# Both groups of heads in one pass of the packing stage, with the first batch ahead of everything else

## The chip, the cores and the metric

The kernel runs on one core of a Trainium2 chip. The metric is the device time of one execution in microseconds (us); lower is better. The engines are named as in the profile: PE is TensorE, which multiplies, PEld its weight loads, DVE is VectorE, ACT is ScalarE, POOL is GpSimd, and SP is the queue that issues nearly all DMAs.

## The reference

Three layers follow each other on 8 batches of 576 tokens with 512 features (8 heads of 64).

```python
# 1. packed attention, per batch and head: p has 32 rows of 64
p_packed = softmax(p @ k.T / 8) @ v
out = softmax(q @ p_packed.T / 8) @ p_packed
# 2. four causal attention experts with 64 features, the two best per token by x @ w_gate
x = concat of the heads
y_e = softmax(causal(x @ wq[e] @ (x @ wk[e]).T / 8)) @ (x @ wv[e]) @ wo[e]
out = sum over the two chosen experts of gate weight * y_e
# 3. token-shift feed-forward
xk = mu_k * x + (1 - mu_k) * x_prev;  xr = mu_r * x + (1 - mu_r) * x_prev
return sigmoid(xr @ w_r) * ((maximum(xk @ w_k, 0) ** 2) @ w_v)
```

## The kernel before, in words

Each batch has two groups of four heads (`NG = 2`). The generator `front(b, g)` takes one group through the packed attention, in nine pieces that end with `yield`: load p, k, v, q (L220 to L229); scores p by k (`heads`, L231), their maximum and exponential (L233 to L238); transposes of the exponentials (L245) and their copy `aT`; the product with v (L254) and its scaling `pp` (L262); the transpose of `pp` and its copy `ppT`; scores q by packed p, transposed on DVE into `st` (L275), maximum `m` (L278), subtraction on POOL (L279), exponential (L280); the product of `ppT` with the weights `wa` of the next layer, kept as a high part `PWh` (L283) and a low part `PWl` (L284); the sums (L287), reciprocal and scaling of `st`; the transpose `a` (L294), kept as `A2h` (ACT) and `A2l` (POOL).

`project` (L374) multiplies `A2h`, `A2l` by `PWh`, `PWl` of both groups into queries and keys, `values` (L319) into values and gate scores. For each expert `soft` makes the causal scores (PE L437), masks and reduces them on DVE (L449) and takes the exponential on ACT (L453); `turn` transposes them (L469, L476), `pair_out` multiplies by the values (L514). Beside this run `fold`, which multiplies `wo` into `w_k` and `w_r` (PE L638), and `vweights`. Both read weights through `decode`: five DVE instructions for each 128 x 256 piece (L568 to L582; the DMA target is `raw`), one on ACT, one on POOL. After the eight batches come `rstage`, `kstage` and `vstage` (L761, L783, L816) over six blocks of columns.

What stands where on an engine is set in two steps. `steps` holds pairs of a time and a generator, and the sorted list calls `next` on them; the times of `front` are `FRONT_T`, shifted by `G1_T` for the second group. The framework then lists the instructions of each engine by its own estimate of when they are ready, and by a priority (`PR` by kind). At run time each engine works through its list in order: an instruction that waits holds all behind it. The DMA queue SP too is such a list.

`pT`, `kT` and the PSUM tiles `big` have two buffers each, the PSUM tiles `one` four. `vn` is two fixed tiles.

Of the kernel before, what the change touches and what calls it, by code (L numbers as in the profile page):

```python
# [23 lines left out]
FRONT_T = [-29.42, -25.75, -23.2, -18.64, -17.38, -14.9, -12.54, -11.97, -8.22]  # L24
G1_T = [1.16, 2.9, 3.77, 1.72, 1.63, 2.21, 3.77, 1.1, 3.2]
VAL_T = [-1.16, -1.09, -0.83, 0.03, 0.74]
PROJ_T = [-1.82, -1.2, 2.22, 2.78]
GROUPS = ((0, 3), (1, 2), (4,))
SOFT_T = [1.34, 2.42, 3.15]
TURN_LAG = [4.17, 4.87, 5.4]  # L30
OUT_LAG = [3.85, 4.62, 7.81]
FOLD_T = [-27.87, 10.28, 107.76]
FOLD_N = 13
V_END = -11.02
WA_AT = -24.33
WR_AT = 8.0
R_LOAD, R_RUN = [14.0, 15.0], [22.0, 28.0]
E_R = "PV"
W_AT = [2.2, 4.2, 5.2]
# [8 lines left out]
PR = {"front": 0, "values": -100, "project": 0, "soft": 0, "turn": 0, "out": 100, "fold": 0, "v": -70, "k": 0, "gates": 0}  # L48
# [7 lines left out]
def kernel(  # L56
# [81 lines left out]
    if True:  # L138
# [17 lines left out]
        vns = [ld.tile([P, NT, 4 * D], F32, name=f"vn{x}", bufs=1) for x in range(2)]  # L156

# [36 lines left out]
        def heads(lhs, rhs, n):  # L194

            ps = big()
            for h in range(4):
                for x in range(2):  # L200
                    nc.tensor.matmul(
                        ps[32 * h : 32 * h + 32, 512 * x : 512 * x + n],
                        lhs[64 * x : 64 * x + 64, 32 * h : 32 * h + 32],
                        rhs[64 * x : 64 * x + 64, h, :],
                        start=True, stop=True,
                    )
            return halves(ps)[:, :, :n]

        def front(b, g):


            if g == 0:
                bats[b] = {
                    n_: bt.tile([P, NG, w], F32R, tag=n_, name=nm(n_))
                    for n_, w in (("A2h", S), ("A2l", S), ("PWh", NQK), ("PWl", NQK))
                }
            bat = bats[b]
            pT = fr.tile([P, P], F32, tag="pT", name=nm("pT"))
            for x in range(2):
                nc.sync.dma_start(pT[64 * x : 64 * x + 64], p[b, g])  # L220
            kT = ld.tile([P, 4, SH], F32, tag="kT", name=nm("kT"))
            nc.sync.dma_start(kT, k[b, g])
            vn = vns[(b * NG + g) % 2]
            nc.sync.dma_start(
                vn[:, : NT - 1, :], v[b, g, : (NT - 1) * P].rearrange("(c p) x -> p c x", p=P)
            )
            nc.sync.dma_start(vn[TAIL:, NT - 1, :], v[b, g, (NT - 1) * P :])
            qT = ld.tile([P, 4, SH], F32, tag="qT", name=nm("qT"))
            nc.sync.dma_start(qT, q[b, g])  # L229
            yield  # L230
            s1 = heads(pT, kT, SH)  # L231
            mx = sm.tile([P, 1], F32, tag="mx1", name=nm("mx1"))
            nc.vector.tensor_reduce(mx, s1, op=ALU.max, axis=AX.XY)  # L233
            nb = sm.tile([P, 1], F32, tag="nb1", name=nm("nb1"))
            nc.vector.tensor_scalar(nb, mx, -SC, None, op0=ALU.mult)
            a1 = fr.tile([P, S], F32, tag="sa", name=nm("a1"), bufs=4)
            su = sm.tile([P, 1], F32, tag="su1", name=nm("su1"))
            nc.scalar.activation(halves(a1), s1, AF.Exp, bias=nb, scale=SC, accum_out=su)  # L238
            nc.vector.tensor_scalar(su, su, EPS, None, op0=ALU.add)
            ri = sm.tile([P, 1], F32, tag="ri1", name=nm("ri1"))  # L240
            nc.vector.reciprocal(ri, su)
            yield
            ps = big()
            for c in range(NT):
                nc.tensor.transpose(  # L245
                    ps[:, c * P : (c + 1) * P], a1[:, start(c) : start(c) + P], ident
                )
            aT = fr.tile([P, NT, P], F32, tag="aT1", name=nm("aT1"), bufs=1)
            evac(E_AT, aT.rearrange("p c q -> p (c q)"), ps[:, : NT * P])
            yield  # L250
            ps = one()
            for c in range(NT):
                for h in range(4):
                    nc.tensor.matmul(  # L254
                        ps[32 * h : 32 * h + 32, :D],
                        aT[:, c, 32 * h : 32 * h + 32],
                        vn[:, c, D * h : D * h + D],
                        start=c == 0, stop=c == NT - 1,
                    )

            pp = fr.tile([P, P], F32, tag="pp", name=nm("pp"))
            nc.vector.tensor_scalar(  # L262
                pp.rearrange("p (x d) -> p x d", x=2),
                ps[:, :D].unsqueeze(1).to_broadcast([P, 2, D]), ri, None, op0=ALU.mult,
            )
            yield
            ps = one()
            nc.tensor.transpose(ps[:, :P], pp, ident)
            ppT = fr.tile([P, P], F32, tag="ppT", name=nm("ppT"))
            evac(E_PPT, ppT, ps[:, :P])  # L270
            yield
            s2 = heads(ppT, qT, SH)
            st = fr.tile([P, S], F32, tag="sa", name=nm("st"), bufs=4)
# [664 lines left out]
```

## Time and profile before

| | |
|---|---|
| median of 3 runs | 873.24 us (871.94 to 873.52) |
| the profiled execution | 872.8 us, its span 871.0 us |
| PE busy | 801.6 us (92% of the span) |
| DVE busy | 548.2 us (63%) |
| POOL, ACT busy | 381.5 us (44%), 377.0 us (43%) |
| DMA | 115.37 MB, mean 132 GB/s; 305 GB/s in the first fortieth of the span |

The span is the time from the first instruction to the last; the run's own time has 1.8 us around it. Busy shares are averages over stages that differ: PE is busy for all of the last 320 us but for about half of the first 44. The clock column (PEclk) gives the share of full speed that was granted; TensorE has two levels, 1.2 and 2.4 GHz. "Idle before" in brackets is the time an engine stood still before an instruction, and what released it.

### The profile page before, as it was taken

The page shows a single profiled execution, that of the slowest core. Times are in us where ns is not written, and L with a number is a line of the kernel's source. Part 1 is how long each engine was busy: PE and PEld are TensorE (multiplying, and loading weights), DVE is VectorE, ACT ScalarE, POOL GpSimd, SP SyncE. Part 2 cuts the span into 40 slices and gives each one's busy share as a digit, 9 for nine tenths or more (in the row PEclk, how much of TensorE's full clock was granted, in tenths as well). Part 3 has the DMA queues.
Part 4 walks back from the last instruction along what each step waited for, and adds up shares of the span by engine and source line. Part 5 has one row for each costly group of instructions (what it writes and reads, how often), then busy time and mean ns, then how long its engine had stood idle before and what let it go on. Part 6 is the DMA issues. An engine that isn't in the chain of part 4 may idle for free. (4 is left out here: it accounts for less than half of the span.)

```text
span 871.0 us, 16389 instructions
## 1 busy us (share of the span) xinstructions
PE 801.6 (92%) x6112; PEld 658.2 (76%) x6112; DVE 548.2 (63%) x1246; ACT 377.0 (43%) x936; POOL 381.5 (44%) x517
## 2 busy tenths in 40 slices
PE   4588999989999889899898978999999999999998
PEld 2285866859678586667777867998889888898896
DVE  2779578694895888986674775554454644554342
ACT  2337657676675856868556453211212112021120
POOL 5773566455763845545443252332423223232230
PEclk9999998999999999999999999999999999999999
DMA  8745461654635467340545875023121131120401
GB/s 305 257 138 167 142 198 63 182 147 128 216 115 161 144 193 212 97 117 24 155 147 186 293 298 209 4 86 108 49 85 62 62 132 49 73 73 1 145 1 72
DMA packets 65903, 115.37 MB, mean 132 GB/s; under 512 B 6048, under 2 KB 45472, under 8 KB 65696
## 3 DMA queue, kind: packets, MB, share of 16 engines
q1 hardware_dynamic: 65824, 114.33, 40.3%
q8 instruction: 48, 0.79, 0.4%
q14 instruction: 31, 0.25, 0.1%
HBM read 71.32 MB, written 33.55 MB: 120 GB/s over the span
## 5 line engine op out<-in xcount | busy, mean ns | idle before, releaser
L816 PE MATMUL one<-wvh,kk 128*128 128x512 f32 x576 | 187.6, 393 | 0.1
L192 POOL TENSOR_TENSOR kk<-y,kk 128x768 fp32r<-128x768 f32 x48 | 89.9, 1873 | 213.7 <-ACT kk L796 213.7
L816 PEld LDWEIGHTS one<-wvh,kk 128*128 128x128 f32 x576 | 107.5, 188 | 22.6 <-DVE rr L821 0.5
L816 PE MATMUL one<-wvl,kk 128*128 128x512 f32 x288 | 113.2, 394 | 0.0
L453 ACT ACTIVATE ms<-ms,nb 64x64 f32<-64x64 f32 (+4 forms) x160 | 89.4, 560 | 32.2 <-DVE nb L449 29.7
L796 ACT CAST kk<-y 128x768 fp32r<-128x768 f32 x48 | 40.1, 836 | 133.0 <-DVE y L794 96.6
L744 DVE TENSOR_TENSOR y<-big,p 128x256 f32<-128x256 f32 x48 | 20.3, 423 | 116.1 <-POOL kk L192 100.3
L185 ACT COPY tb<-one 64x128 f32<-64x128 f32 (+5 forms) x208 | 65.9, 356 | 22.1 <-PE one L469 19.5
L791 ACT COPY p<-big 128x256 f32<-128x256 f32 x48 | 17.9, 373 | 125.0 <-PE big L783 106.2
L514 PE MATMUL one<-tb,vg 128*64 128x320 f32 (+4 forms) x448 | 62.1, 379 | 3.2 <-ACT p L767 2.3
L816 PEld LDWEIGHTS one<-wvl,kk 128*128 128x128 f32 x288 | 54.1, 188 | 10.4
L449 DVE CUSTOM_DVE_ANT_0 ms<-one,mstrip 64x64 f32<-64x64 f32 (+3 forms) x128 | 51.3, 420 | 13.1 <-PE one L437 10.9
L469 PE MATMUL one<-ident,ms 128*128 128x128 f32 x320 | 55.6, 286 | 3.7 <-ACT ms L453 2.4
L514 PEld LDWEIGHTS one<-tb,vg 128*64 128x64 f32 x448 | 37.2, 142 | 26.0 <-issue 3.6
L469 PEld LDWEIGHTS one<-ident,ms 128*128 128x128 f32 x320 | 37.3, 143 | 23.1 <-issue 10.7
L821 DVE TENSOR_TENSOR rr<-one,rr 128x512 f32<-128x512 f32 x36 | 23.1, 683 | 41.2 <-PE one L816 41.1
L794 DVE SCALAR_TENSOR_TENSOR y<-y 128x768 f32<-128x768 f32 x48 | 48.0, 999 | 1.6
L181 POOL TENSOR_SCALAR dh<-dl 128x2048 fp32r<-128x2048 f32 x10 | 19.2, 1923 | 65.2 <-DMA dl<-dscr 65.2
L437 PE MATMUL one<-ks,qs 128*128 128x64 f32 (+3 forms) x128 | 41.0, 345 | 5.6 <-DVE tb L187 2.6
L578 POOL TENSOR_TENSOR dcx<-dcx,dce 128x256 f32<-128x256 f32 x40 | 29.3, 733 | 38.2 <-DVE dce L575 32.7
L476 PE MATMUL one<-ident,ms 128*128 128x128 f32 x160 | 35.6, 287 | 9.9 <-DVE nb L449 6.0
L739 DVE TENSOR_TENSOR dl<-dl,dh 128x2048 fp32r<-128x2048 f32 x10 | 29.7, 2971 | 18.2 <-POOL dh L181 18.2
(172 smaller groups left out, 2086.2 us busy)
## 6 DMA issues: line engine op xcount, KB each, us to landing
dl<-dscr SPq DMA_DIRECT2D x10, 1024.0 KB, 6.1
kT<-in_k_dram SPq DMA_DIRECT2D x16, 576.0 KB, 4.6
qT<-in_q_dram SPq DMA_DIRECT2D x16, 576.0 KB, 5.4
rscr<-rr SPq DMA_DIRECT2D x12, 768.0 KB, 4.1
rr<-rscr SPq DMA_DIRECT2D x12, 768.0 KB, 4.3
out_dram<-rr SPq DMA_DIRECT2D x11, 768.0 KB, 3.3
vn<-in_v_dram SPq DMA_DIRECT2D x16, 512.0 KB, 5.0
dscr<-dt SPq DMA_DIRECT2D x16, 384.0 KB, 4.6
```

Of the source, the lines that this page charges most:

```text
L185: nc.scalar.copy(o, x)
L192: nc.gpsimd.tensor_tensor(o, x, y, op=op)
L437: nc.tensor.matmul(ps[:, po : po + kn], qs[:, i * P : i * P + P], keys[:, ko : ko + kn], start=x == 0, stop=x == 1,)
L449: nc.vector.tensor_tensor_reduce(halves(mv) if last else mv, sv, halves(mk) if last else mk, op0=ALU.add, op1=ALU.min, scale=-SC, scalar=3 ...
L453: nc.scalar.activation(mv, mv, AF.Exp, bias=nb[p0:], scale=-1.0, accum_out=bat["sums"][p0:, i, e : e + 1],)
L469: nc.tensor.transpose(ps[:, at + j * P : at + (j + 1) * P], ms[:, j * P : (j + 1) * P], ident)
L476: nc.tensor.transpose(pd[:, at + P * x : at + P * x + P], ms[:, start(i) : start(i) + P], ident)
L514: nc.tensor.matmul(av[64 * ee : 64 * ee + 64, qo - lo : hi - lo], vg[:, j, HD * (2 * ep + ee) : HD * (2 * ep + ee + 1)], tslice(tabs[ee], ...
L739: nc.vector.tensor_sub(dl, f32(dl), f32(dh))
L794: nc.vector.scalar_tensor_tensor(y, y, 0.0, y, op0=ALU.max, op1=ALU.mult)
L796: nc.scalar.copy(kk[:, 0], y)
L816: nc.tensor.matmul(ps, kk[:, a, x, t0 : t0 + P], wres["v"][b][:, f, :], start=n == 0, stop=n == 3 * NFT - 1,)
```

## The change

`front(b)` now takes both groups through each piece together: every tile is a list of two, and each step is written for group 0 and then for group 1. `st`, `a1`, `aT` and `a2` share four buffers of one tag. `tc.issue_after` asks that PE work of a piece stand behind that of the piece before. For the first batch three things differ: its priority is 1000 in place of 0 (`PR0`); the four small loads of p are issued by ACT and not by SP; and the subtraction, the scaling and the `A2l` subtraction go to DVE and not to POOL (`light`), which moves six instructions. At the start DVE clears a one-column tile `warm`, ACT takes its exponential, and PE multiplies 16 times a 128 x 128 piece of zeros of `mstrip` (`WARM`), all at the highest priority. In `pair_out` the two experts of a pair change places. The times of many steps are other numbers.

```diff
-FRONT_T = [-29.42, -25.75, -23.2, -18.64, -17.38, -14.9, -12.54, -11.97, -8.22]
-G1_T = [1.16, 2.9, 3.77, 1.72, 1.63, 2.21, 3.77, 1.1, 3.2]
+FRONT_T = [-25.49, -24.5, -21.5, -17.8, -16.5, -14.0, -11.0, -10.5, -7.0]
...
+PR0, WARM = 1000, 16
...
+        with tc.high_priority(offset=10000):
+
+            warm = const.tile([P, 1], F32, name="warm")
+            nc.vector.memset(warm, 0.0)
+            nc.scalar.activation(warm, warm, AF.Exp)
+            wps = one()
+            for _ in range(WARM):
+                nc.tensor.matmul(wps[:, :P], mstrip[:, :P], mstrip[:, P : 2 * P], start=True, stop=True)
...
+            gs = range(NG)
+            light = nc.gpsimd if b else nc.vector
+
+            def wide():
+                return [fr.tile([P, NT * P], F32, tag="sa", name=nm("sa"), bufs=4) for _ in gs]
...
+                for x in range(2):
+                    (nc.sync if b else nc.scalar).dma_start(pT[g][64 * x : 64 * x + 64], p[b, g])
+                kT.append(ld.tile([P, 4, SH], F32, tag="kT", name=nm("kT")))
+                nc.sync.dma_start(kT[g], k[b, g])
...
+            s1 = [heads(pT[g], kT[g], SH)[0] for g in gs]
+            a1, mx, nb, su, ri = wide(), small("mx1"), small("nb1"), small("su1"), small("ri1")
+            for g in gs:
+                nc.vector.tensor_reduce(mx[g], s1[g], op=ALU.max, axis=AX.XY)
+                nc.vector.tensor_scalar(nb[g], mx[g], -SC, None, op0=ALU.mult)
+                nc.scalar.activation(
+                    halves(a1[g][:, :S]), s1[g], AF.Exp, bias=nb[g], scale=SC, accum_out=su[g]
+                )
+            yield
+            for g in gs:
+                nc.vector.tensor_scalar(su[g], su[g], EPS, None, op0=ALU.add)
+                nc.vector.reciprocal(ri[g], su[g])
...
+            for g in gs:
+                for hf in range(2):
+                    nc.vector.transpose(st[g][:, SH * hf : SH * hf + SH], s2[g][:, hf, :])
+                nc.vector.tensor_reduce(m2[g], st3[g], op=ALU.max, axis=AX.X)
+                light.tensor_tensor(
+                    st3[g], st3[g], m2[g].unsqueeze(2).to_broadcast([P, NCB, NPK]), op=ALU.subtract
+                )
+                nc.scalar.activation(st[g][:, :S], st[g][:, :S], AF.Exp, scale=SC)
...
+                light.tensor_tensor(
+                    st3[g], st3[g], r_[g].unsqueeze(2).to_broadcast([P, NCB, NPK]), op=ALU.mult
+                )
+            yield
+            a2 = wide()
+            for g in gs:
+                nc.vector.transpose(a2[g][:, :S], st[g][:, :S])
+                evac(E_AH, bat["A2h"][:, g, :], a2[g][:, :S])
+                light.tensor_tensor(
+                    bat["A2l"][:, g, :], a2[g][:, :S], f32(bat["A2h"][:, g, :]), op=ALU.subtract
+                )
...
-                    for ee in range(2):
+                    for ee in (1, 0):
...
-            for g in range(NG):
-                add("front", front(b, g), [t0 + t + g * G1_T[i] for i, t in enumerate(FRONT_T)])
+            add("front", front(b), [t0 + t for t in FRONT_T], None if b else PR0)
```

Three places in the engines' lists show what this moves. Line numbers of the changed kernel are its own; `sa` there is what was `a`, `aT` or `st`.

First, the head of SP's list before, up to the first weight piece `raw`:

```order
L220 DMA pT_130<-in_p_dram 64x128 x2
L222 DMA kT_133<-in_k_dram 128x1152
L224 DMA vn_122<-in_v_dram 128x4x256
L227 DMA vn_122<-in_v_dram 64x256
L229 DMA qT_137<-in_q_dram 128x1152
L220 DMA pT_139<-in_p_dram 64x128 x2
```

and of the change:

```order
L240 DMA kT_170<-in_k_dram 128x1152
L240 DMA kT_175<-in_k_dram 128x1152
L243 DMA vn_122<-in_v_dram 128x4x256
L247 DMA vn_122<-in_v_dram 64x256
L249 DMA qT_179<-in_q_dram 128x1152
L243 DMA vn_123<-in_v_dram 128x4x256
```

The loads of p have left the list, and both loads of k stand first; behind these rows the same loads follow in the same order as before, up to `wa` and `raw`.

Second, DVE in the first batch from the first piece of `raw` on, before:

```order
L568 TENSOR_SCALAR dce_233<-raw_230 128x256
L571 SCALAR_TENSOR_TENSOR dcx_232<-raw_230,dce_233 128x256
L574 TENSOR_SCALAR dce_233<-dcx_232 128x256
L275 STREAM_TRANSPOSE st_342<-big_333 128x288 x2
L575 SCALAR_TENSOR_TENSOR dce_233<-raw_230,dce_233 128x256
L278 TENSOR_REDUCE m_57_345<-st_342 128x18
L582 SCALAR_TENSOR_TENSOR sq_229<-sq_229,dcx_232 128x256
```

and of the change, where `sa_370` and `sa_371` are `st` of the two groups and `big_352`, `big_361` their scores:

```order
L305 STREAM_TRANSPOSE sa_370<-big_352 128x288 x2
L306 TENSOR_REDUCE m_59_372<-sa_370 128x18
L305 STREAM_TRANSPOSE sa_371<-big_361 128x288 x2
L606 TENSOR_SCALAR dce_241<-raw_238 128x256
L307 TENSOR_TENSOR sa_370<-sa_370,m_59_372 128x576
L306 TENSOR_REDUCE m_60_373<-sa_371 128x18
L609 SCALAR_TENSOR_TENSOR dcx_240<-raw_238,dce_241 128x256
L317 TENSOR_TENSOR PWl_166<-big_398,PWh_165 128x772
```

The transposes and the first maximum have gone ahead of the first decode instruction, all later work of the batch still stands behind it, and the subtractions are new in DVE's list. From `dce_241<-raw_238` to the second `A2l` the changed list has 30 instructions.

Third, DVE in the fifth batch, where the next scores of `soft` (ISA `ms`) meet the maxima of the two groups, before:

```order
L233 TENSOR_REDUCE mx_558_2708<-big_2699 128x1
L575 SCALAR_TENSOR_TENSOR dce_3408<-raw_3405,dce_3408 128x256
L235 TENSOR_SCALAR nb_559_2710<-mx_558_2708 128x1
L294 STREAM_TRANSPOSE a_566_2733<-st_2477 128x576
L239 TENSOR_SCALAR su_561_2713<-su_561_2713 128x1
L241 RECIPROCAL ri_562_2716<-su_561_2713 128x1
L568 TENSOR_SCALAR dce_3501<-raw_3498 128x256
L531 TENSOR_TENSOR cb_2724<-one_2668,cb_2724 128x320
L531 TENSOR_TENSOR cb_2724<-one_2679,cb_2724 128x256
L233 TENSOR_REDUCE mx_577_2794<-big_2785 128x1
L449 ISA ms_117,nb_571_2754<-one_2749,mstrip 64x64
```

and of the change:

```order
L254 TENSOR_REDUCE mx_562_2754<-big_2734 128x1
L255 TENSOR_SCALAR nb_564_2756<-mx_562_2754 128x1
L254 TENSOR_REDUCE mx_563_2755<-big_2743 128x1
L261 TENSOR_SCALAR su_566_2758<-su_566_2758 128x1
L255 TENSOR_SCALAR nb_565_2757<-mx_563_2755 128x1
L262 RECIPROCAL ri_568_2760<-su_566_2758 128x1
L261 TENSOR_SCALAR su_567_2759<-su_567_2759 128x1
L262 RECIPROCAL ri_569_2761<-su_567_2759 128x1
L487 ISA ms_117,nb_575_2802<-one_2797,mstrip 64x64
```

Here the scores of `soft` stand behind the sums `su` of both groups, where before they stood behind one.

## Rows read from the trace of the kernel before

**Rows 1.** Busy time of each engine by stretch (from:to and length; instructions in brackets).
```profile
0.00:43.74 43.74, 21.19 (x237) 10.10 (x237) 22.13 (x54) 11.97 (x22) 30.14 (x65) 1.00 0.82 282
43.74:65.01 21.27, 18.53 (x118) 18.09 (x119) 16.85 (x29) 7.66 (x18) 15.86 (x25) 0.92 0.47 135
65.01:92.00 26.99, 23.72 (x273) 15.21 (x271) 26.49 (x85) 19.49 (x59) 12.44 (x17) 0.94 0.49 151
92.00:300.00 208.00, 195.09 (x1926) 153.44 (x1927) 152.93 (x449) 135.56 (x390) 121.44 (x217) 0.96 0.51 150
...
550.00:800.00 250.00, 250.00 (x1520) 222.41 (x1519) 122.82 (x176) 44.35 (x74) 79.14 (x42) 1.00 0.19 68
```

**Rows 2.** Timeline of PE: start, length, instructions, and idle time before them.
```profile
6.16 1.21 PE L201 MATMUL big<-kT,pT 64*32 64x288 f32 x16 [6.16 <-DMA kT<-in_k_dram]
10.77 1.30 PE L245 MATMUL big<-ident,a 128*128 128x128 f32 x5 [3.40 <-ACT a L238]
...
19.82 1.21 PE L201 MATMUL big<-qT,ppT 64*32 64x288 f32 x16
...
43.74 0.85 PE L374 MATMUL big<-A2h,PWh 128*128 128x288 f32 x2 [1.53 <-ACT a L238]
...
59.87 0.53 PE L374 MATMUL big<-A2h,PWh 128*128 128x288 f32 x2 [2.37 <-DVE l L389]
...
88.09 0.71 PE L201 MATMUL big<-kT,pT 64*32 64x288 f32 x16
...
133.34 0.42 PE L437 MATMUL one<-ks,qs 128*128 128x64 f32 x1 [1.98 <-DVE tb L187]
```

**Rows 3.** Timeline of the DMA queue SP: start and length of the issue.
```profile
0.73 1.22 SPq L220 DMA_DIRECT2D pT<-in_p_dram  x2
2.00 0.58 SPq L222 DMA_DIRECT2D kT<-in_k_dram  x1
...
11.87 2.12 SPq L564 DMA_DIRECT2D raw<-in_w_k_dram  x2
```

**Rows 4.** Short stretches; last three columns granted clock, DMA share, GB/s.
```profile
6.00:36.00 30.00, 16.60 (x210) 7.72 (x211) 16.69 (x38) 8.95 (x16) 17.14 (x41) 1.00 1.03 360
...
62.00:64.00 2.00, 2.00 (x12) 2.00 (x11) 1.91 (x3) 1.14 (x3) 1.73 (x4) 0.50 0.63 178
```

**Rows 5.** Timeline of DVE in the first batch.
```profile
21.05 0.29 DVE L568 TENSOR_SCALAR dce<-raw 128x256 int32<-128x256 int32 x1 [0.74 <-DMA raw<-in_w_k_dram]
...
30.48 1.36 DVE L582 SCALAR_TENSOR_TENSOR sq<-sq,dcx 128x256 f32<-128x256 f32 x1 [0.74 <-POOL dcx L578]
```

**Rows 6.** Timeline of POOL in the first batch.
```profile
30.41 1.15 POOL L192 TENSOR_TENSOR st<-st,r 128x576 f32<-128x576 f32 x1
...
42.49 1.44 POOL L192 TENSOR_TENSOR A2l<-a,A2h 128x576 fp32r<-128x576 f32 x1
```

**Rows 7.** DVE instructions by line and shape: busy us, mean ns.
```profile
L794 DVE SCALAR_TENSOR_TENSOR y<-y 128x768 f32<-128x768 f32 x48 | 48.0, 999 | 1.6
...
L582 DVE SCALAR_TENSOR_TENSOR sq<-sq,dcx 128x256 f32<-128x256 f32 x40 | 24.0, 599 | 9.9 <-POOL dcx L578 5.8 <-ACT sq L581 4.1
...
L574 DVE TENSOR_SCALAR dce<-dcx 128x256 int32<-128x256 int32 x40 | 18.0, 451 | 0.5
...
L284 DVE TENSOR_TENSOR PWl<-big,PWh 128x772 fp32r<-128x772 f32 x16 | 15.1, 941 | 1.6 <-ACT PWh L283 1.5
...
L294 DVE STREAM_TRANSPOSE a<-st 128x576 f32<-128x576 f32 x16 | 12.2, 763 | 1.9 <-POOL st L192 1.8
...
L278 DVE TENSOR_REDUCE m<-st 128x18 f32<-128x576 f32 x16 | 11.9, 745 | 0.2
...
L290 DVE RECIPROCAL r<-s 128x18 f32<-128x18 f32 x16 | 3.9, 246 | 0.3 <-POOL s L288 0.3
...
L239 DVE TENSOR_SCALAR su<-su 128x1 f32<-128x1 f32 x16 | 2.3, 143 | 7.0 <-ACT a L238 7.0
```

**Rows 8.** Timeline of ACT before the first exponential.
```profile
8.50 1.28 ACT L238 ACT_TABLE_LOAD   x1 [8.50 <-DVE nb L235]
```

More of the change, by code (lines that the diff above doesn't have):

```diff
@@ L250, in front @@
             yield
+            ppT = [fr.tile([P, P], F32, tag="ppT", name=nm("ppT")) for _ in gs]
             ps = one()
[L252 to L261, printed above, removed]
@@ L291, in front @@
[L291 to L296 removed]
+            with tc.issue_after(last.ins):
+                for g in gs:
+                    last = nc.tensor.transpose(ps[:, P * g : P * g + P], pp[g], ident)
+                    evac(E_PPT, ppT[g], ps[:, P * g : P * g + P])
@@ new lines, in front @@
+            yield
+            with tc.issue_after(last.ins):
+                s2, last = zip(*(heads(ppT[g], qT[g], SH) for g in gs))
+            st = wide()
+            m2 = small("m2", NCB)
+            st3 = [t[:, :S].rearrange("p (c n) -> p c n", n=NPK) for t in st]
+            for g in gs:
+                for hf in range(2):
[3 more added lines that the diff above has]
+                    st3[g], st3[g], m2[g].unsqueeze(2).to_broadcast([P, NCB, NPK]), op=ALU.subtract
+                )
+                nc.scalar.activation(st[g][:, :S], st[g][:, :S], AF.Exp, scale=SC)
@@ new lines, in front @@
+            yield
+            with tc.issue_after(last[-1].ins):
+                ps = [heads(ppT[g], wa[:, 4 * g : 4 * g + 4, :], NQK // 2)[0] for g in gs]
+            for g in gs:
+                h = bat["PWh"][:, g, :]
+                nc.scalar.copy(halves(h), ps[g])
+                nc.vector.tensor_sub(halves(bat["PWl"][:, g, :]), ps[g], halves(f32(h)))
+            yield
+            s_, r_ = small("s2", NCB), small("r2", NCB)
+            for g in gs:
+                nc.vector.tensor_reduce(s_[g], st3[g], op=ALU.add, axis=AX.X)
+                nc.gpsimd.tensor_scalar(s_[g], s_[g], EPS, 0.0, op0=ALU.add, op1=ALU.add)
+                nc.vector.reciprocal(r_[g], s_[g])
+                light.tensor_tensor(
+                    st3[g], st3[g], r_[g].unsqueeze(2).to_broadcast([P, NCB, NPK]), op=ALU.mult
+                )
@@ L827, in vstage, with add @@
                     )
-        last = U * (B - 1) + max(t + max(0, d) for t, d in zip(FRONT_T, G1_T)) + 0.1
+        last = U * (B - 1) + max(FRONT_T) + 0.1
         prio = {}
-        def add(kind, gen, times):
-            prio[gen] = PR[kind]
+        def add(kind, gen, times, prior=None):
+            prio[gen] = PR[kind] if prior is None else prior
             for t in times:
```

133 lines of the change are left out of this document (53 added, 80 removed).

## The prediction

> **What bounds the kernel now.** I read the table of stretches first [rows 1]. From 550 us on PE is busy for 250 of 250 us, and nothing in the change touches that part. From 92 to 300 us PE stands still for 208.00 - 195.09 = 12.9 us. The first 43.74 us are another matter: PE is busy for 21.19 of them, so 22.6 us are lost there, more than in all of the next 250. So I look at who is late in the first batch, and at what a restart 1 us earlier is worth behind it.
>
> The timeline of PE gives the chain of the first batch [rows 2]: the first product starts at 6.16 when k lands, the scores of q at 19.82, and at 43.74 the projections begin to run without a break. That row names ACT, but ACT's instruction was done before; what ends there is POOL's second `A2l`, 42.49 + 1.44 [rows 6]. From there to the first causal scores, at 65.01, 2.74 us of 21.27 are idle [rows 1], 2.37 of them in one wait for DVE [rows 2]. From 65 to 92 DVE is busy for 26.49 of 26.99 us: there DVE is the bound, not PE.
>
> Why does the chain take until 43.74? Two views answer. In the short stretches the 16 DMA engines are full from 6 to 36 us, share 1.03 at 360 GB/s [rows 4]. And DVE stands until 21.05 for the first piece of `raw`, which sits behind all loads of the batch in the DMA queue and, in DVE's list, ahead of the batch's own transposes [rows 3, 5]. So the chain has a floor made of transfers up to 21 us, and then a DVE list in which batch work and decode work are mixed.
>
> **The change, part by part.** *Loads.* The first large load (k) was issued at 2.00 us, behind two loads of p, and is now issued at about 0.73 [rows 3]. With the DMA engines full behind it, all that follows should land 1.27 us earlier, `raw` at 21.05 - 1.27 = 19.8. The bounds are 19.8 and 21.05, the latter if the transfers themselves are the limit and the order of issue is not; I take 19.8, since no transfer ran before the first large issue.
>
> The Trainium skill speaks against more than that: by DMA: Bandwidth & Descriptors, section Issuing engines are not separate DMA queues, DMAs issued by ACT and by SP run on the same 16 engines, and another issuer saves only the time of issue. The trace agrees with full engines at share 1.03.
>
> *Table.* The load of the exponential's table, 1.28 us, stood in the chain at 8.50 [rows 8] and now runs while k is on its way. It then sits between the loads of p on ACT, so the second half of p is issued some 2 us later than the first; k needs 4.16 us from its issue (2.00 to 6.16), which covers that.
>
> *Warm-up.* The first product took 1.21 us at 6.16 and the same one 0.71 at 88.09 [rows 2]: TensorE is at its lower level (1.2 GHz) in the first stage, although the column of granted clock reads 1.00 there. The 16 products have no row. Below, five transposes of the same size took 1.30, 0.26 each [rows 2], so 16 take 4.2 us; above, an ordinary product shows as two records (8 calls of `heads` give x16), so 8.3. Begun at about 1.6 us (an estimate: DVE must have cleared two tiles), they end between 5.8 and 9.9, and the first product, which could start at 0.73 + 4.16 = 4.9, stands behind them. Their gain is a faster clock for as long as it lasts; after an idle time of 2.37 us it fell to 0.50 at 62 us [rows 2, 4], and the chain has such gaps. I count gain and loss as equal.
>
> *What the earlier chain is worth until `raw` lands.* Before, 13.66 us passed from the first product to the scores of q [rows 2]. With 1.28 for the table gone that is 12.4, and part of it was waiting behind the other group. A first product at 4.9 gives scores at 17.3, one at 7.5 (between the warm-up's ends) 19.9 at the latest. DVE then needs two transposes and a maximum, some 2.3 us. So this part meets the landing of `raw` at 19.8 within about a microsecond; I take 20.1 as the time at which DVE passes the first decode instruction. Table and warm-up are thus hidden behind the transfers; without that cover the table alone would be worth its 1.28 us.
>
> *DVE from there to the second `A2l`.* The changed list has 30 instructions. Seven of 576 columns (one maximum, two sums, two maxima of the next batch, two transposes) cost 0.745 to 0.763, together 5.25. Two `PWl` cost 0.941, together 1.9. Nine decode instructions cost 0.451 to 0.599, together 4.6. Six short ones cost 0.143 to 0.246, together 1.1. All [rows 7].
>
> The six that come from POOL have no row on DVE. Below: `y` with both operands in SBUF took 999 ns for 768 columns [rows 7], which is 0.75 for 576. Above: at 30.48 an instruction with a mean of 0.599 took 1.36, ending with the POOL instruction that began at 30.41 and took 1.15 [rows 5, 6, 7]. I take 0.9, nearer to the lower end, since POOL's own pieces here are shorter now that these six have left it: 5.4. The sum is 5.25 + 1.9 + 4.6 + 1.1 + 5.4 = 18.2 us (17.3 to 21.0), so the second `A2l` is ready at 20.1 + 18.2 = 38.3 and not at 43.74: **5.4 us** earlier (at the least favourable ends 21.05 + 21.0 = 42.1, which leaves 1.7 us).
>
> The Trainium skill has the reason for the upper end: by Advanced Engine Details and Errata, section VectorE Performance Modes, the second SBUF port of VectorE is shared with GpSimd, and the two block each other. The trace shows such a case at 30.48. If all six were held so, the sum would be 21.0 and the gain 2.6 us; the mean of 0.599 for 40 decode instructions that meet POOL too speaks for less.
>
> *After the chain.* PE's work to the first causal scores is the same, 18.53 us busy in 21.27 [rows 1]. The wait of 2.37 may go, since the projections of all four kinds now stand together; I count half, +1.2. Against that, 34 decode instructions stand ahead of the first wide score pass on DVE where 37 did; the three are made up where DVE has only 0.5 us to spare [rows 1]: -1.5. Together -0.3.
>
> *All later batches.* The instructions are the same in number and engine; PE's list is the same work in nearly the same order. Nothing is removed. I count 0, and the risk below.
>
> *Sum.* 5.4 - 0.3 = 5.1 us; against the profiled execution's 872.8 that is 867.7, against the median of the runs, 873.24, it is 868.1. I say **867.8**.
>
> **The rivals.** *DVE runs without a gap.* From 43.74 to 92 us DVE is idle for 4.42 + 0.50 = 4.9 us [rows 1]. With the batch's work at hand earlier these could fill: 867.8 - 4.9 = 862.9. For it speaks that the order between this batch's steps is freer; against it, that each wait there is for a cast or a product just issued.
>
> *The start gains nothing to speak of.* The transfers are the floor: `raw` lands at 21.05 as before, and POOL holds up the six instructions. Then the gain is 1.7 us or less, 871 to 872. For it speaks the DMA share of 1.03 up to 36 us; against it, that the second group's chain on DVE and POOL took until 43.74, long after.
>
> *The pairing costs in every later batch (slower).* With both groups in one step, `su` of both groups, which wait for ACT's exponential, stand ahead of the next score pass in DVE's list (the fifth batch, above). Behind that pass wait the exponential on ACT, the transposes on PE. An exponential and the short instructions between add 0.3 to 1 us, and a full stall of this kind cost 1.98 at 133.34 [rows 2]. Seven batches have it: it eats the gain of 5.4 from 0.77 us each; at 1 us the time is 874.8, at 1.98 it is 867.8 + 13.9 = 881.7. For it speaks that PE already waits there for DVE; against it, that in some batches the pass stands between the two sums, and that PE has other work in its list.
>
> **How the numbers follow.** A measurement of this kernel tells about 0.2% (1.75 us) from no change. I give the forecast 0.58 (865 to 870.5), the gapless case 0.13 (860 to 865), no gain at the start 0.12 (870.5 to 873), the pairing's cost 0.17 (871 to 881). The range of 861 to 874.5 leaves about a tenth above and less below. Faster than 871.5: all of the first two and a fourth of the third, 0.74. Same: most of the third and a little of the fourth, 0.12. Slower than 875: most of what is left, 0.14.
>
> **What would show it.** In the profile after: `raw` landing near 19.8 and the first decode instruction on DVE there; the six moved instructions at 0.75 to 1.36 each on DVE; the projections running without a break from about 38; first causal scores near 60; the stretch from 92 us on with the idle time of before. I am wrong if the second heads are late because the warm-up or p holds the first product beyond 9, if `raw` does not move, or if PE's idle time in the later batches grows by more than 0.77 us each.

## The result, and the profile after

The changed kernel takes 881.32 us (median of 4 runs, 879.16 to 886.01) against 872.59 us for the kernel before on the same chip: ratio 1.0109, 95% interval 1.0061 to 1.0157. It is slower by 1.1%, where I had forecast 0.6% faster. The profiled execution took 879.62 us with a span of 877.8, 6.8 more than before.

The stretches of [rows 1] in the changed kernel, and one more:

```profile
0.00:43.74 43.74, 25.44 (x282) 16.65 (x282) 23.59 (x60) 12.94 (x25) 23.56 (x59) 0.69 0.86 283
43.74:65.01 21.27, 18.03 (x195) 16.86 (x194) 14.74 (x34) 8.05 (x20) 13.77 (x22) 0.92 0.49 131
65.01:92.00 26.99, 21.41 (x190) 14.10 (x179) 24.54 (x75) 17.57 (x54) 14.43 (x19) 0.87 0.47 147
92.00:300.00 208.00, 183.20 (x1921) 147.06 (x1921) 155.47 (x456) 137.06 (x391) 121.81 (x218) 0.99 0.51 150
...
530.00:560.00 30.00, 23.50 (x156) 20.68 (x155) 13.61 (x20) 11.31 (x14) 15.61 (x7) 1.00 0.57 195
550.00:800.00 250.00, 250.00 (x1518) 224.49 (x1519) 124.41 (x180) 45.20 (x76) 79.41 (x42) 1.00 0.19 68
```

From 92 to 300 us PE stands still for 24.8 us where it stood for 12.9, but that is a poor measure of the loss, as the next table shows. At 530 to 560 us it stands still for 6.5 us, where it did for 2.2 before:

```profile
530.00:560.00 30.00, 27.78 (x194) 25.58 (x193) 16.11 (x23) 9.40 (x14) 7.71 (x5) 1.00 0.28 106
```

PE in the first batch, to be held against [rows 2]:

```profile
7.07 0.71 PE L209 MATMUL big<-kT,pT 64*32 64x288 f32 x16
...
32.65 0.58 PE L676 MATMUL one<-wh,wo 128*128 128x256 f32 x1 [3.19 <-POOL wh L189]
...
37.90 1.01 PE L676 MATMUL one<-wh,wo 128*128 128x256 f32 x3 [2.81 <-POOL wo L189]
...
44.06 0.53 PE L412 MATMUL big<-A2h,PWh 128*128 128x288 f32 x2 [0.28 <-ACT sa L193]
```

And DVE, against [rows 5] and [rows 6] (`A2l` is its work now):

```profile
15.68 0.17 DVE L636 TENSOR_SCALAR om<-om 128x8 f32<-128x8 f32 x1 [5.24 <-DMA om<-in_mu_r_dram]
...
21.88 0.30 DVE L606 TENSOR_SCALAR dce<-raw 128x256 int32<-128x256 int32 x1 [0.53 <-DMA raw<-in_w_k_dram]
22.09 0.75 DVE L307 TENSOR_TENSOR sa<-sa,m 128x576 f32<-128x576 f32 x1
22.76 0.75 DVE L306 TENSOR_REDUCE m<-sa 128x18 f32<-128x576 f32 x1
...
29.23 1.87 DVE L324 TENSOR_TENSOR sa<-sa,r 128x576 f32<-128x576 f32 x2
...
35.34 0.88 DVE L332 TENSOR_TENSOR A2l<-sa,A2h 128x576 fp32r<-128x576 f32 x1
```

The first heads run at the faster level (0.71, the length of a later batch in [rows 2]). `raw` is not earlier but 0.83 us later than the 21.05 of [rows 5]; its issue has moved from the 11.87 of [rows 3] to 12.58, though the first k is issued at 0.73:

```profile
0.73 0.86 SPq L240 DMA_DIRECT2D kT<-in_k_dram  x2
...
12.58 1.06 SPq L602 DMA_DIRECT2D raw<-in_w_k_dram  x2
```

The second `A2l` is done at 36.22, 7.7 us before the 43.93 of [rows 6]. So the chain up to there came out better than forecast, and the kernel is slower all the same. To see where it turns I follow one event through the trace: the start of DVE's score pass over 448 columns (it occurs once for each expert; in the changed kernel the first begins at 64.8).

```
start, us                     before  changed  c_firstee  p_old   h1
batch 1, first expert           66.1     64.8       64.1   64.6   64.2
batch 1, third expert           84.2     79.0       82.3   78.9   81.0
batch 1, fourth expert          97.1     96.1       96.3   96.0   95.8
batch 3, first expert          166.2    168.7      163.9  168.4  171.5
batch 5, first expert          269.8    271.7      267.3  275.4  278.5
batch 6, first expert          324.9    327.5      321.8  327.9  332.4
batch 6, fourth expert         364.0    365.9      354.0  364.0  369.2
batch 7, first expert          378.2    383.3      369.4  382.5  389.5
batch 8, first expert          420.8    427.2      412.6  428.8  430.0
first product of kstage        529.6    532.1      519.8  536.4  537.6
end of the last one           846.7    854.0      837.9  854.8  855.7
```

The last three columns are experiments, explained below. The changed kernel leads by 5.2 us at the third expert, by 1.0 at the fourth; by the third batch it is behind, and another 4.8 us (7.3 against 2.5) are lost between the first and last product of `kstage`. The 7.7 us at the second `A2l` have become 1.3 us at the first score pass, where the forecast had first causal scores near 60.

### The profile page after: what moved, and what is told of

It reads as the page before. It is cut to its first block, busy times and chain, and to the rows that moved or that the text cites. A ratio compares the mean times of both kernels' runs of the same rounds, so it can differ in the third digit from the quotient of the medians.

```text
span 877.8 us, 16445 instructions
## 1 busy us (share of the span) xinstructions
PE 789.2 (90%) x6144; PEld 660.1 (75%) x6144; DVE 552.9 (63%) x1253; ACT 377.4 (43%) x937; POOL 374.6 (43%) x511
## 5 line engine op out<-in xcount | busy, mean ns | idle before, releaser
L507 PE MATMUL one<-ident,ms 128*128 128x128 f32 x320 | 55.8, 288 | 7.6 <-ACT ms L491 4.4
L487 DVE CUSTOM_DVE_ANT_0 ms<-one,mstrip 64x64 f32<-64x64 f32 (+3 forms) x128 | 51.2, 420 | 9.4 <-PE one L475 7.5
L552 PE MATMUL one<-tb,vg 128*64 128x320 f32 (+4 forms) x448 | 51.2, 374 | 3.9 <-ACT tb L193 3.1
L552 PEld LDWEIGHTS one<-tb,vg 128*64 128x64 f32 x448 | 30.1, 141 | 27.3 <-ACT tb L193 7.0
L821 PE MATMUL big<-dh,wk0h 128*128 128x256 f32 x192 | 39.7, 284 | 5.9 <-DVE y L784 3.0
L676 PE MATMUL one<-wh,wo 128*128 128x256 f32 x192 | 34.8, 301 | 10.3 <-POOL wh L189 5.4
```

Of the source, the lines that this page charges most:

```text
L487: nc.vector.tensor_tensor_reduce(halves(mv) if last else mv, sv, halves(mk) if last else mk, op0=ALU.add, op1=ALU.min, scale=-SC, scalar=3 ...
L507: nc.tensor.transpose(ps[:, at + j * P : at + (j + 1) * P], ms[:, j * P : (j + 1) * P], ident)
L552: nc.tensor.matmul(av[64 * ee : 64 * ee + 64, qo - lo : hi - lo], vg[:, j, HD * (2 * ep + ee) : HD * (2 * ep + ee + 1)], tslice(tabs[ee], ...
L676: nc.tensor.matmul(ps, a[:, c, t * P : t * P + P], bb[:, c, :], start=i == 0, stop=i == 3 * NDT - 1,)
L821: nc.tensor.matmul(ps[:, o : o + EB], wpart("k0" if f < 4 else "k1", s, wx, t)[:, f % 4 * P : f % 4 * P + P], dx[:, NS * t + s, :], start= ...
```

## The experiments

All ratios are to the kernel before, run on the same chip in the same session, with 95% intervals.

**The last stages.** The diff's `W_AT`, `WR_AT`, `R_LOAD`, `R_RUN` and third `OUT_LAG`, undone in the changed kernel (a_tail), and made alone in the kernel before (b_tail):

```diff
...
-W_AT = [2.94, 5.14, 6.34]
+W_AT = [2.2, 4.2, 5.2]
```

This is a line of a_tail's edit; b_tail makes the same lines the other way round.

> The changed kernel with the times of the last stages as before: W_AT, WR_AT, R_LOAD, R_RUN and the third OUT_LAG. Theory (the tail): in the changed kernel the loads of the last weights stand behind four more stores in SP's list, and PE stands still for 6.5 us from 525 to 560 where it stood still for 2.2; put back, that idle time falls to about 2 us and the time by about 4, to 877. Rival (the pairing costs in every batch and the tail only passes on what came late): the time stays within 1 us of 881.

> The kernel before with only the changed times of the last stages. Theory (the tail): the same four stores move ahead of the weight loads, and the time rises by about 4 us, from 872.6 to some 877, with PE idle near 6 us between the last batch and the second k block. Rival (the pairing): within 1 us of 872.6.

Measured: a_tail 880.03 us, 1.0077 (1.0049 to 1.0106); b_tail 877.90 us, 1.0062 (1.0039 to 1.0085). In SP's list of the changed kernel the loads of `wvl` now stand behind four stores that wait for their data one by one:

```profile
507.30 21.82 SPq L810 DMA_DIRECT2D rscr<-rr  x4
529.16 2.62 SPq L726 DMA_DIRECT2D wvl<-vscr  x4
```

Two engines hand the delay on to PE. ACT's casts of these weights wait for the loads and hold a copy `p`, on which hang DVE's `y` and, behind it, a buffer of `big`: PE waits 2.52 us there, where the longest wait for `y` before was 0.49. POOL's split of these weights holds `kk`, for which PE waits another 0.63 at 548.12:

```profile
538.07 1.05 ACT L193 CAST wvh<-wvl 128x1024 fp32r<-128x1024 f32 x1 [0.73 <-DMA wvl<-vscr]
...
540.79 0.42 DVE L782 TENSOR_TENSOR y<-big,p 128x256 f32<-128x256 f32 x1 [3.96 <-ACT p L829]
...
542.54 0.48 PE L821 MATMUL big<-dh,wk0h 128*128 128x256 f32 x2 [2.52 <-DVE y L784]
```

```profile
536.15 10.12 POOL L730 TENSOR_TENSOR wvl<-wvl,wvh 128x1024 fp32r<-128x1024 f32 x4 [23.30 <-ACT wvh L193]
546.24 1.83 POOL L200 TENSOR_TENSOR kk<-y,kk 128x768 fp32r<-128x768 f32 x1
```

In b_tail the same loads are issued at 526.29; in the kernel before they are ahead of the four stores:

```profile
503.01 3.33 SPq L688 DMA_DIRECT2D wvl<-vscr  x4
```

The time between the first product of `kstage` and the last of `vstage` was 342.2 us in b_tail and 342.0 in the changed kernel, 337.7 in the kernel before and 338.0 in a_tail. So the new times cost 4 to 5 us in the last stages. b_tail came out as the theory said (877). a_tail did not: its last stages are 4 us shorter, but its `kstage` began at 537.6 and not at 532.1, so that most of it was lost before.

**The first batch alone.** c_first leaves the new stage, priority, warm-up and DVE steps to the first batch; the seven later ones go one group at a time, with the old times. Three things of the change stay with all batches: the four buffers shared by `st`, `a1`, `aT` and `a2`, the new time of the load of `wa` (`WA_AT`), and the first of `FOLD_T`. c_firstee also puts the two experts of a pair back into their old order.

```diff
-            add("front", front(b), [t0 + t for t in FRONT_T], None if b else PR0)
+            if b == 0:
+                add("front", front(b), FRONT_T, PR0)
+            else:
+                for g in range(NG):
+                    add("front", front1(b, g), [t0 + t + g * G1_T[i] for i, t in enumerate(FRONT1_T)])
...
-                    for ee in (1, 0):
+                    for ee in range(2):
```

> The paired stage for the first batch alone, with its priority, the three steps on DVE, the loads of p by ACT and the warm-up; all later batches go through the stage of before, one group at a time, and all other times are those of before but the fold's first. Theory (the start gains what the second A2l gains, 5 us, and the rest of the change costs): 868 to 870. Rival (the gain of the start is lost behind the first batch whatever follows, as the score passes at 97 us show): 871 to 874.

> The paired stage for the first batch alone with all else as before, the experts' order too. Theory (the start gains 3 to 5 us and the exchange cost the rest of the 3.7 us that the run with the exchange stood above before): 868 to 870. Rival (what the start gains is given back within the next batches, whatever the experts' order): 873 to 877.

Measured: c_first 876.94 us, 1.0039 (1.0021 to 1.0057); c_firstee **866.29 us, 0.9933 (0.9908 to 0.9958)**. It beats both kernels. c_first is slower than both ranges of its expectation, c_firstee faster than both of its own. The start of c_firstee is that of the changed kernel to within 0.7 us at the first pass in the table, and at the fifth batch it leads by 2.5 us, where the changed kernel is 1.9 behind. In its profiled execution (863.7 us, its fastest) the lead grows from 3.1 us at the start of the sixth batch to 9.9 at that batch's last expert. The lists differ there in many rows; which of them counts I did not try.

The step in the sixth batch is no accident of one execution: the four variants of c_firstee below (c_nowarm, c_om, c_pool, c_noprio) have leads of 0.0 to 3.4 us at its first expert and 6.7 to 8.3 at its last. So most of what c_firstee gains does not come from the first batch, and every run that is held against c_firstee below is held against this step too: p_old, f_new, c_first, h1 and h2 gain 0.6 to 3.0 us on the kernel before in that batch, c_firstee and its four variants 4.9 to 6.8.

**The exchange of the experts.** I had not looked at it. In the kernel before (b_ee) and undone in the changed one (a_ee):

```diff
...
-                    for ee in range(2):
+                    for ee in (1, 0):
...
```

This is b_ee's edit; a_ee's is the reverse.

> The kernel before with the two experts of a pair exchanged in the products with the values, nothing else. In the changed kernel these products keep PE busy for 51.2 us instead of 62.1 at the same mean duration. Theory (the exchange lets products of the two experts run side by side and takes 11 us of busy time from PE, but where PE waits for others anyway that only becomes idle time): busy time of these products near 51, PE's idle time between 44 and 400 us up by some 10, and the time within 2 us of 873. Rival (PE is the bound there, so its time counts): 865 or less. Second rival (the exchange moves the engines' lists to a worse order): 876 or more.

> The changed kernel with the two experts in the old order. Theory (the exchange only turns busy time of PE into idle time): busy time of these products back at 62, the time within 2 us of 881. Rival (PE's time counts): 890. Second rival (the exchange made the order worse): 878 or less.

Measured: b_ee 882.02 us, 1.0109 (1.0087 to 1.0131); a_ee 880.37 us, 1.0081 (1.0055 to 1.0106). Both theories had the busy time of these products wrong: over all shapes it is 62.1 us in the kernel before and 55.2 in b_ee, 51.2 in the changed kernel and 56.2 in a_ee. b_ee fell to its second rival (a worse order), a_ee stayed within its theory's time. The widest of these products, by line and shape, first in the kernel before:

```profile
L514 PE MATMUL one<-tb,vg 128*64 128x320 f32 x192 | 42.6, 469 | 3.2 <-ACT p L767 2.3 <-ACT tb L185 0.9
```

in b_ee:

```profile
L514 PE MATMUL one<-tb,vg 128*64 128x320 f32 x192 | 34.5, 501 | 6.7 <-ACT tb L185 6.7
```

and in c_firstee and c_first:

```profile
L644 PE MATMUL one<-tb,vg 128*64 128x320 f32 x192 | 39.4, 442 | 4.8 <-ACT p L897 2.3 <-ACT tb L195 1.3 <-DVE nb L579 1.0
```

```profile
L644 PE MATMUL one<-tb,vg 128*64 128x320 f32 x192 | 34.2, 498 | 12.5 <-ACT tb L195 12.5
```

Busy time of this shape falls by 8 and 5 us, though each product takes 7 and 13% longer (the products of the two experts lie more side by side), but the wait for `tb` rises from 0.9 to 6.7 and from 1.3 to 12.5 us. In the old list some products of the pair's first expert run before the second expert's `tb` is there; exchanged, the first product in the list is one that needs it. It cost 9.5 us in b_ee (1.09%) and 9.3 between c_firstee and c_first; in the changed kernel, where this wait is 3.1 us, 2.4, which the intervals do not tell from nothing. The Trainium skill, Perfetto Trace Analysis, section Identifying the Most-Contended Engine, says that the matmul busy share is not a good measure of how close TensorE is to its limit; this trace agrees: the busy time fell and the time rose.

**The later batches.** p_old pairs the groups in all batches, with the old order of the experts and the old times of all other steps (only the step that swaps in the last weights, which hangs on the end of the packing stage, comes a little earlier). f_new is c_firstee with the changed kernel's times of `values`, `soft`, `turn`, `fold` and `v`. a_eetail is the changed kernel with a_tail's and a_ee's edits together.

```diff
-VAL_T = [-1.16, -1.09, -0.83, 0.03, 0.74]
+VAL_T = [-1.16, -1.09, -0.83, 0.03, 0.59]
...
-SOFT_T = [1.34, 2.42, 3.15]
+SOFT_T = [1.34, 2.54, 3.15]
...
```

These are lines of f_new's edit of c_firstee.

> Both groups together in all batches, with the experts in the old order and all times of later steps as before (values, soft, turn, out, v, last stages); only the times of the packing stage itself are the new ones. It differs from the 866.3 us run in the packing stage of the seven later batches alone. Theory (the pairing costs in every later batch, about 1 us each or more): 873 to 880. Rival (the pairing costs nothing, the new times of the other steps do): 866 to 869.

> The pairing in the first batch alone, old order of the experts, old times of the last stages, but the new times of values, soft, turn, fold and v. It differs from the 866.3 us run in these times alone. Theory (the pairing costs, not these times): 866 to 869. Rival (these times cost): 873 to 880.

> The changed kernel with the experts in the old order and the old times of the last stages (both together). If the costs add up (about 1 for the exchange here, 4.2 for the last stages): 876. If the times of the last stages only move the delay, as in the run with these alone: 880.

Measured: p_old 879.96 us, 1.0073 (1.0050 to 1.0096); f_new 874.26 us, 1.0013 (0.9994 to 1.0032); a_eetail 876.87 us, 1.0046 (1.0026 to 1.0067). From c_firstee to p_old it is 1.4%, 12 us for seven batches, **1.7 us each on the average**. It does not come evenly: in the table p_old is 0.5 us behind c_firstee at the first batch, 4.5 at the third, 8.1 at the fifth, 13.1 at the seventh and 16.2 at the eighth (c_firstee's profiled execution is its fastest, p_old's its slowest, so the traces are further apart than the medians). The new times are worth 2.4 us to the paired stage (p_old to a_eetail) and cost 7 where it is not paired (c_firstee to f_new). So pairing and times are no two separate costs: with the old times the pairing costs 12.2 us, with the new ones (f_new to a_eetail) 2.9, where the intervals just meet. What stands firm is both together, c_firstee to a_eetail: 9.9 us. Both theories were half right: p_old fell in its theory's range, f_new in its rival's.

By which wait? In p_old the longest sum of PE's waits is one for `tb`, 6.6 us (4.3 in c_firstee). New is that PE waits at the causal scores, in `big`, for the packing stage to give a buffer back (total, times, longest, from 92 to 430 us):

```profile
PE one L507 <- ACT tb L193: 6.6, 3, 3.6
PE big L475 <- ACT sa L256: 5.9, 4, 2.5
...
PE big L475 <- DVE PWl L317: 2.7, 3, 1.1
```

In c_firstee and in the kernel before there is no such wait in `big`. `big` has two buffers, and a pair fills both. So p_split keeps the pair but makes the second group's scores of p and its product with `wa` later steps of their own, with the first pieces a little earlier:

```diff
...
+            if b:
+                scores(0)
+                yield
+                scores(1)
...
```

> The kernel paired in all batches with the old times (880.0 us), but in the seven later batches the second group's scores of p and its product with wa are a step of their own, later than the first group's, and the first pieces come somewhat earlier; all else stays paired. Theory (the pair fills both buffers of big, and the causal scores behind wait until PWl or the exponential frees one): the two waits of the causal scores in big go, and the time falls by most of the 13 us, to 867 to 873. Rival (the pairing costs elsewhere, by the order on DVE and ACT): those waits go but the time stays at 877 or more.

Measured: 881.50 us, 1.0093 (1.0066 to 1.0120). The profiled execution is its fastest, 875.4 us. The two waits are gone from it (0.3 us left), others stand in their place:

```profile
PE one L502 <- DMA ks<-ks: 5.3, 4, 2.7
PE big L439 <- DVE kl L454: 3.6, 2, 2.7
PE one L534 <- ACT ms L518: 3.3, 2, 2.6
PE big L502 <- DVE sa L320: 3.0, 2, 1.8
```

My theory fell for the two waits that I had named: they are real and do not carry the cost. The buffers are not ruled out altogether: the scores of q are still a pair in p_split, and the last row is a wait for a buffer that holds them. The last two runs pair only one half of the stage in the later batches, h1 the half up to `pp`, h2 the half behind it.

```diff
...
-                    add("front", front1(b, g), [t0 + t + g * G1_T[i] for i, t in enumerate(FRONT1_T)])
+                    add("front", fronta(b, g), [t0 + t + g * G1_T[i] for i, t in enumerate(FRONT1_T[:4])])
+                add("front", frontb(b), [t0 + t for t in FRONT_T[4:]])
```

This is from h2's edit of c_firstee.

> The 866.3 us kernel with the first half of the stage (loads, scores of p, exponential, transposes, product with v, pp) paired in the seven later batches too, the second half one group at a time at the old times. Theory (the first half carries the cost: two exponentials of 576 columns and two copies in a row on ACT, su ahead of the score passes on DVE): 873 to 880. Rival (the second half, with two pairs of wide steps on DVE and POOL): 866 to 869. If both halves cost, some 873 here and in the next run.

> The 866.3 us kernel with the second half of the stage (from the transpose of pp on) paired in the seven later batches too, the first half one group at a time at the old times. Theory (the first half carries the cost): 866 to 869. Rival (the second half does): 873 to 880.

Measured: h1 882.78 us, 1.0126 (1.0097 to 1.0155); h2 874.19 us, 1.0015 (0.9994 to 1.0037). The first half alone costs no less than the whole, 1.9% above c_firstee, the second 0.8%. They don't add up to the 1.4% of both, and neither expectation held: h1 is slower than its theory, and h2 fell in its rival's range. In p_old, h1 and h2 the pieces also have the new times of the packing stage (loads at -25.49 in place of -29.42), so these runs do not tell the pairing from its times. p_split, with its loads at -29.0 and its first scores at the old -25.75, was no faster, which speaks against the loads.

**The parts of the start.** The warm-up alone in the kernel before (b_warm), taken out of the changed kernel (a_nowarm) and out of c_firstee (c_nowarm); `light` on POOL (c_pool) and priority 0 (c_noprio) in c_firstee; and `om` moved (c_om):

```diff
...
-            nc.vector.tensor_scalar(om, om, -1.0, 1.0, op0=ALU.mult, op1=ALU.add)
+            nc.gpsimd.tensor_scalar(om, om, -1.0, 1.0, op0=ALU.mult, op1=ALU.add)
```

> The kernel before with only the cleared tile, the early exponential and the 16 products. Theory (first products at the faster clock and no table load in the chain, but the transfers are the floor): first heads near 7 us, score pass of the first expert within 1 us of 66.1, time within 1.5 us of 873. Rival (the early clock carries over): 3 us lower or more.

> The changed kernel without the cleared tile, the early exponential and the 16 products. Theory (warm-up and its clock are worth little, the transfers are the floor): within 2 us of 881, with the first heads near 5 us at 1.2 us, raw where it was. Rival (the early warm-up brings the clock's later fall to 0.50 at 84 to 92 us): that fall is gone or smaller, and the time is 3 us or more lower, 878 or less.

> The 866.3 us kernel (pairing in the first batch alone) without the cleared tile, the early exponential and the 16 products. Theory (table and warm-up are hidden by the transfers, gain and loss alike): 866.3 within 2 us. Rival (the faster clock in the first products is needed): 869 or more, the scores of q later.

> The 866.3 us kernel with subtraction, scaling and A2l of the first batch on POOL again, as in the kernel before. Theory (these six at 0.83 each on DVE against some 1.3 on POOL, in the chain): the second A2l 3 us later or more, 868 to 871. Rival (the projections wait for the first products of fold anyway): 866.3 within 1.5 us.

> The 866.3 us kernel with the first batch's priority 0. Theory (the order set by the priority is what brings the chain ahead of decode work on DVE): second A2l 2 us later or more, 868 to 872. Rival (the estimate of the framework gives nearly the same order): within 1.5 us.

> The 866.3 us kernel with one instruction moved: the sign change of om goes from DVE, where it stands ahead of the scaling pp and waits 5 us for its transfer, to POOL. Theory (that wait is the start's floor now): pp at 10.5 to 13 instead of 15.5, the scores of q by 15, the first score pass 2 to 3 us earlier and the time 864 or less. Rival (raw at 21.8 and wa at 21 are the floor just behind it, so nothing is gained): score passes where they were, 866.3 within 1.5 us.

Measured: b_warm 876.32 us, 1.0047 (1.0028 to 1.0066); a_nowarm 879.98 us, 1.0071 (1.0047 to 1.0094); c_nowarm 865.61 us, 0.9923 (0.9903 to 0.9942); c_pool 868.93 us, 0.9960 (0.9942 to 0.9977); c_noprio 869.15 us, 0.9965 (0.9952 to 0.9978); c_om 866.93 us, 0.9929 (0.9904 to 0.9955). The warm-up gains nothing anywhere, and in b_warm it costs 4.1 us, more than the 1.5 of its theory. There the first score pass comes 4.5 us later, at 70.6, and DVE shows why: `om`'s instruction now stands ahead of the second group's maximum; first the kernel before, then b_warm:

```profile
13.32 0.76 DVE L233 TENSOR_REDUCE mx<-big 128x1 f32<-128x576 f32 x1 [2.31 <-PE big L201]
```

```profile
16.19 0.17 DVE L607 TENSOR_SCALAR om<-om 128x8 f32<-128x8 f32 x1 [5.52 <-DMA om<-in_mu_r_dram]
16.27 0.75 DVE L242 TENSOR_REDUCE mx<-big 128x1 f32<-128x576 f32 x1
```

In c_om that wait is off DVE and the scores of q run at 14.91 instead of 16.89, but PE then waits 5.33 us for `wa`, and DVE 3.91 for `raw`:

```profile
21.44 2.83 PE L211 MATMUL big<-wa,ppT 64*32 64x386 f32 x32 [5.33 <-DMA wa<-in_w_in_dram]
```

So the landing of `wa` and `raw` near 22 us is the floor, and what stands before it is free. The rival of a_nowarm was half right: the granted clock from 84 to 92 us, 0.59 in the changed kernel (0.50, the lower level, from 84 to 90), is 1.00 without the warm-up. But it is 1.00 in c_firstee with the warm-up too, and the 3.3 us between a_nowarm and the changed kernel are within the intervals.

Against c_firstee, c_pool is 2.4 us slower and c_noprio 2.8, by ratios whose intervals overlap a little with its own. The second `A2l` in c_firstee, c_pool and c_noprio:

```profile
34.69 0.95 DVE L334 TENSOR_TENSOR A2l<-sa,A2h 128x576 fp32r<-128x576 f32 x1
```

```profile
34.45 1.41 POOL L334 TENSOR_TENSOR A2l<-sa,A2h 128x576 fp32r<-128x576 f32 x1
```

```profile
43.89 1.28 DVE L334 TENSOR_TENSOR A2l<-sa,A2h 128x576 fp32r<-128x576 f32 x1
```

With the six instructions on POOL it is done at 35.86 and not at 35.64: c_pool's theory (3 us later or more) has the time and not the reason. In c_noprio it is done at 45.17, 9.5 us later than in c_firstee and 1.2 later than in the kernel before, and that kernel is still 0.35% faster than the kernel before (0.9952 to 0.9978). In c_nowarm it is done at 39.32, and the time is that of c_firstee. So the time at which the second `A2l` is done, on which the forecast was built, decides little of the whole.

## Why the prediction was wrong

**The sum.** In us of 873, along one order of the runs:

```
step                                       ratio after it   us
first batch's start, shared buffers,
times of wa and first fold (c_firstee)         0.9933      -5.8
later batches paired (p_old)                   1.0073     +12.2
times of the other steps (a_eetail)            1.0046      -2.4
times of the last stages (a_ee)                1.0081      +3.1
experts exchanged (changed kernel)             1.0109      +2.4
```

The first two steps are clear of the noise. For the other three the intervals overlap; the last two parts are clear where they are made alone in the kernel before (b_tail, b_ee). By another order of the runs, through f_new, the times cost 7.0 and the pairing behind them 2.9.

**Loads: wrong.** `raw` was to land at 19.8 and landed at 21.88, beyond my upper bound of 21.05. An earlier first issue moved nothing: the issue of `raw` itself came 0.7 us later. It cost little, since the next term was too large. (Small loads of p did run before the first large one, unlike my reason for 19.8.)

**Table, warm-up: right here.** The table's load now runs at 1.29 and not at 8.50 [rows 8]:

```profile
1.29 1.28 ACT L161 ACT_TABLE_LOAD   x1 [1.29 <-PEq L964]
```

 The products end near 7.1, inside my 5.8 to 9.9, and with or without them the time is the same (0.9933 and 0.9923). Alone in the kernel before they cost 4.1 us by the order on DVE, which I had not costed.

**DVE to the second `A2l`: right in kind, the sum too large.** The six moved instructions took 0.75, 0.75, 1.87 for two, 0.74 and 0.88, together 4.99 (5.4 forecast), with no stall behind POOL. But the same 30 instructions took 14.3 us and not 18.2. Nine of decode took 3.2 and not 4.6; and I added durations, where the next instruction starts before the last one ends: 0.75 at 22.09, the next at 22.76. Their durations add up to 16.3 us, 1.9 more than passed. And the move to DVE, which is 5.4 of my 18.2 us, was not needed: c_pool reaches the second `A2l` within 0.2 us of c_firstee.

**After the chain (-0.3): a step that failed.** I let the lead at `A2l` pass on whole but for 0.3 us. Of its 7.7 us only 1.3 are left at the first score pass, a loss of 6.4. PE waits 3.19 and 2.81 us for the first products of `fold`, which stand ahead of the projections in its list; of the second wait 1.7 us lie behind the end of `A2l` at 36.22. After it PE turns to the next batch's transposes and to `fold` in between, and its projections run without a break from 44.06, no earlier than the 43.74 of before [rows 2]. That c_firstee gains 5.8 us, near my sum of 5.1, is therefore luck: by the table some 2 to 3 of them come from the first batch, the rest from the sixth, and c_noprio gains 3.1 with an `A2l` that is later than before.

**All later batches, "I count 0": the step that failed most.** It is 9.9 us for the pairing and the new times together, 12.2 for the pairing at the old times. I argued from the number of instructions and from PE's list; both are nearly the same, and it was no argument. My third rival had the case, and I gave it 0.17. Its size is right for p_old alone (0.77 us each decides, it is 1.7), and that the changed kernel, at 881.3, lands just beyond its upper end of 881 is partly chance, since the last stages and the exchange are in it too. Its mechanism, `su` ahead of the score pass, is not what the trace shows: DVE's waits at `su` from 100 to 410 us are 2.8 us in the kernel before and 3.4 in the changed one.

**"Nothing in the change touches that part": wrong.** The diff shows new `W_AT`; I read the last 320 us as bound by PE and asked no further which transfers must be there when they begin: 3.1 us here, 5.4 alone.

**The exchange was not costed at all**: 2.4 us here, 9.5 alone.

**The chances.** They don't quite agree with each other: a range with about a tenth above 874.5 goes badly with 0.14 for slower than 875.

What stays open: the mechanism by which the paired stage costs up to 12 us, and that by which c_firstee and its variants gain in the sixth batch. The two waits of p_old in `big` are excluded, `su` is not borne out, and no wait of PE has been shown to carry the cost. Not tried are the shared buffers by themselves, the pair of the scores of q, and a wait on ACT: its exponential of those scores waits for POOL's subtraction for 11.2 us in p_old from 92 to 430 us, 8.3 in h1, 5.0 in c_firstee and 3.3 in the kernel before.

## What to carry to other kernels

Where engines work through lists in a fixed order, an edit that changes no instruction can cost 1%: give each edit of an order its own run, as the best version here keeps the first step of the sum and leaves out the other four. Two such edits need not add up (pairing and times, above). Ask of a pair of steps that is put together what else needs its turn in between, and of a queue which store that waits stands ahead of which load. A lead at one point of a chain is a gain only if it is still there a batch later, and a time near the forecast is no proof of its path.

## What I had not expected of the hardware

PE's idle time from 92 to 300 us rose by 11.9 us in the changed kernel while its 15th to 20th score passes came only 0.6 to 3.4 us late. Busy time can fall without a gain of time: for all shapes of the products with the values it is 62.1 us before and 51.2 after, 448 of them at a mean of 379 and 374 ns, so that more of them lie side by side. About half of that is the exchange (56.2 in a_ee). But it explains little of the idle time: a_ee, with the old order, stands still for 23.9 us in that window, the changed kernel for 24.8.
